# Six score bursts a batch in place of five, one of them inside a down pair

## The chip, the cores and the metric

The kernel runs on one core of one Trainium2 chip. Its time is the device time of one execution in microseconds (us); smaller is better. The engines are TensorE (PE, with its weight loads shown as PEld), VectorE (DVE), ScalarE (ACT), GpSimd (POOL) and SyncE (SP), each with its own queue of instructions, which it takes in order. Matmul results land in PSUM, which has eight banks.

## The reference

Sigmoid attention over 8 batches, 12 heads, 448 tokens and head size 64 is followed by a gated feed-forward network on all 3584 tokens (width 768, inner width 1536). Inputs and outputs are fp32; the kernel multiplies in fp16.

```python
scores = scale * np.matmul(q, k.transpose(0, 1, 3, 2)) - np.log(S)
attn = 1.0 / (1.0 + np.exp(-scores))
x = np.matmul(attn, v)              # then to (tokens, heads * head size)
gate = np.maximum(x @ w_gate, 0.0)
val = x @ w_val
out = gate * val @ w_out
```

There is no softmax, so a score needs one sigmoid and no sum over its row.

## The kernel before

**Attention.** A batch has three groups of four heads, and each group's keys come in seven chunks. A *unit* (`qk_unit`, line 292) is the scores of one group and one chunk: four 64x64 matmuls of 448 columns that run side by side in the four quarters of the array (`qk`, line 232). It fills two banks, and two sigmoids on ACT (line 187) carry them to an fp16 tile PT. A *value product* (`pv`, line 250) takes the seven PT tiles of one group: 28 such matmuls into two banks, which DVE scales and copies out as xT (line 184). A batch has 21 units, in order of group and chunk, and three value products.

**Bursts.** The units are cut into *bursts* by the list `cuts` (lines 699 to 706). Between bursts stands one piece of feed-forward work. `pv_at` names the bursts that hold a value product and the place in them: after two units of the burst. From batch 3 on there are five bursts, of 4, 4, 4, 4 and 5 units; the first, third and fifth hold a value product (the first one that of the last group of the batch before). Batch 2 has six bursts of 4, 3, 4, 3, 4 and 3 units, with the value products in those of four.

**Feed-forward work.** The first batches use plain products (`gv`, one strip of gate and value, line 309). From batch 2 on, work comes from a deque (`push_group`, line 668) that holds, for each two batches, six gate-and-value pairs, one plain down product (`down`, line 346) and three down pairs. `next_work` (line 682) takes one after each burst. Pairs form a 2x2 block product from seven smaller products in a reordered form (`gv_pair`, line 510; `down_pair`, line 423); sums of operands are made ahead on DVE by `prepare`, batch sums by `batch_sums`. With five pieces of work a batch, an even batch b gives y (the last down pair), w, w, w, w, and an odd one w, w, t, y, y; batch 3 has three plain strips, then t and y.

**A down pair** makes two tiles of 128 tokens, y1 and y2, from three banks b, c and a. Each product is six matmuls of 384 columns. In order: A11 x B11 into b, copied by DVE (line 416; ACT in the last pieces of the kernel) to the low half of y1; S1 x T1 into c, copied by ACT (line 421) to the high half of y2; S2 x T2 added into b, copied by ACT to the high half of y1; A12 x B21 into a, added to y1 low by DVE (line 437); S3 x T3 added into b, added to y2 high by DVE; S4 x B22 added into c, added to y1 high by DVE; the stores of y1; then A22 x T4 added into b, copied by ACT to the low half of y2; the stores of y2. The jobs handed in as `beside` follow the first copy: the DVE copies and SP transposes that bring the next keys and queries into place (`dma_transposes`, line 211), POOL's loads of the next batch, and batch sums.

**Banks.** `bank` (line 76) hands out the eight PSUM banks in a ring, the one that was given out longest ago first. `later` (line 84) moves banks to the ring's end by their place: the argument 7 is the last of the ring, 0 the first. A down pair ends with the order a, c, b behind the five others, a gate-and-value pair with a, a, c, c, b, b behind the two others. A matmul that writes a bank waits for the engine that read it last.

**Order.** The schedule is written by hand: instructions stand on each engine's queue in the order in which the program issues them.

Of the kernel before, what the change touches and what calls it, by code (L numbers as in the profile page):

```python
# [17 lines left out]
def kernel(  # L18
# [10 lines left out]
    nc = tc.nc  # L29

    B, H, S, D = q.shape
    DM, DF = moe_w_gate.shape
# [43 lines left out]
    def bank(name, shape=(P, 512), dtype=FP32):  # L76
        pool, tag = free[0]
        free.rotate(-1)
        return pool.tile(list(shape), dtype, tag=tag, name=name)
# [4 lines left out]
    def later(order):  # L84
        keys = [free[i - 8] for i in order]
        for key in keys:
            free.remove(key)
            free.append(key)
# [211 lines left out]
    def pv_group(b, g):  # L300
        pv(b, g, 0, S, [PT_tiles.pop((b, g, c))[:, :, 0:S] for c in range(NCH)])
# [32 lines left out]
    def store(g, t, ysb, m0, m1, engines):  # L334
        for i, eng in enumerate(engines):
            j = 2 * t + i
            b, c = 2 * g + j // NCH, j % NCH
            dst = out[b * S : (b + 1) * S, m0:m1].rearrange("(t c) m -> c t m", c=NCH)[c]
            eng.dma_start(dst, ysb[64 * i : 64 * i + 64, m0:m1])
# [24 lines left out]
    HF, HM, HD = NFC // 2, DM // 2, NDC // 2  # L364
# [55 lines left out]
    def scaled_act(o, ps):  # L420
        nc.scalar.activation(o, ps[:, 0:HM], AF.Copy, scale=OUT_SCALE)  # L421

    def down_pair(g, p, beside, then, last, first_copy):
        A11, A12, S3, A22 = token_blocks(g, p)
        S1, S2, S4 = sums.pop(("y", g, p))
        T1, T2, T3, T4 = (late["T"][:, i] for i in range(4))
        B11, B21, B22 = wo[:, 0:HF, 0:HM], wo[:, HF:NFC, 0:HM], wo[:, HF:NFC, HM:DM]
        y1, y2 = (ysbp.tile([P, DM], FP32, tag="ysb", name="ysb") for _ in range(2))
        lo, hi = slice(0, HM), slice(HM, DM)
        b, c, a = bank("u"), bank("y12"), bank("y11")  # L430
        later((7, 6, 5))

        def product(ps, A, W, first=True):
            products([(ps, HM, HF, A, W, first)])

        def plus(o, ps):
            nc.vector.scalar_tensor_tensor(  # L437
                out=o, in0=ps[:, 0:HM], scalar=OUT_SCALE, in1=o, op0=AOP.mult, op1=AOP.add
            )

        product(b, A11, B11)
        first_copy(y1[:, lo], b)
        beside()
        product(c, S1, T1)
        scaled_act(y2[:, hi], c)
        product(b, S2, T2, False)
        scaled_act(y1[:, hi], b)
        product(a, A12, B21)
        plus(y1[:, lo], a)
        if last:  # L450
            store(g, 2 * p, y1, 0, HM, (nc.sync, nc.sync))
        product(b, S3, T3, False)
        plus(y2[:, hi], b)
        if last:
            scaled_act(y2[:, lo], b)
            store(g, 2 * p + 1, y2, HM, DM, (nc.sync, nc.scalar))
        product(c, S4, B22, False)
        plus(y1[:, hi], c)
        if last:
            store(g, 2 * p, y1, HM, DM, (nc.sync, nc.scalar))  # L460
        else:
            store(g, 2 * p, y1, 0, DM, (nc.sync, nc.sync))
        then()
        if last:
            for m0 in (0, HM // 2):
                m1 = m0 + HM // 2
                d = bank("y21")
                products([(d, HM // 2, HF, A22, T4[:, :, m0:m1], True)])
                nc.vector.scalar_tensor_tensor(
                    out=y2[:, m0:m1], in0=d[:, 0 : HM // 2], scalar=OUT_SCALE, in1=y2[:, m0:m1],  # L470
                    op0=AOP.mult, op1=AOP.add,
                )
            store(g, 2 * p + 1, y2, 0, HM, (nc.sync, nc.scalar))
        else:
            product(b, A22, T4, False)
            scaled_act(y2[:, lo], b)
            store(g, 2 * p + 1, y2, 0, DM, (nc.sync, nc.sync))
# [165 lines left out]
    order = [(g, c) for g in range(NG) for c in range(NCH)]  # L643
# [12 lines left out]
    def both(b, g):  # L656
        pe_transposes(b, g, 0)
        pe_transposes(b, g, 1)
# [7 lines left out]
    work = deque()  # L666
# [12 lines left out]
            elif kind == "y":  # L679
                token_sums(g, i)  # L680

    def next_work(jobs=(), alone=False, first_act=False):
        kind, g, i = work.popleft()

        def beside():
            for job in jobs:
                job()

        if kind == "y":
            down_pair(g, i, beside, prepare, not work, scaled_act if alone or first_act else scaled)  # L690
        elif kind == "w":
            gv_pair(g, i, lambda: (prepare(), beside()), nc.scalar.copy if alone else nc.vector.tensor_copy)
        else:
            beside()
            prepare()
            down(g, i)

    ffn_mix(1, [(1, lambda: both(1, 0))])
    for b in range(1, B):
        if b == 1:  # L700
            cuts, pv_at = (0, 3, 6, 9, 13, 17, 21), {3: (0, 2), 5: (1, 2)}
        elif b == 2:
            cuts, pv_at = (0, 4, 7, 11, 14, 18, 21), {0: (-1, 2), 2: (0, 2), 4: (1, 2)}
        else:
            cuts, pv_at = (0, 4, 8, 12, 16, 21), {0: (-1, 2), 2: (0, 2), 4: (1, 2)}
        count = len(cuts) - 1
        hooks = {}
        if b == 1:
            mix = (3, 3, 3, 3, 3, 2)
            hooks = {  # L710
                1: [(1, lambda: both(1, 1))],
                3: [(1, lambda: both(1, 2))],
                4: [(3, lambda: dma_transposes(2, 0))],
                5: [(2, lambda: dma_transposes(2, 1)), (0, late_loads)],
            }
        elif b == 2:
            mix = (2, 2, 1, 1, 1, 2)
            hooks = {
                2: [(0, prepare)],
                4: [(0, lambda: weight_sums(0))],  # L720
                5: [(1, lambda: weight_sums(1)), (0, lambda: weight_sums(2))],
            }
            open_late()
        elif b == 3:
            mix = (1, 1, 1, 0, 0)
        else:
            mix = (0,) * count
        for m in range(count):
            jobs = []
            for i, (g, c) in enumerate(order[cuts[m] : cuts[m + 1]]):  # L730
                if m in pv_at and i == pv_at[m][1]:
                    if m == 0:
                        pv_finish(b - 1)
                        if b == 2:
                            push_group(0)
                        elif b % 2 == 0:
                            push_group(b // 2 - 1)
                    else:
                        pv_group(b, pv_at[m][0])
                qk_unit(b, g, c)  # L740
            if m == 0 and b > 2:
                jobs.append(lambda: dma_transposes(b, 2))
            if b == 2 and m == count - 1:
                jobs.append(lambda: (dma_transposes(3, 0), dma_transposes(3, 1)))
            elif b == 3 and m == count - 1:
                jobs.append(lambda: (dma_transposes(4, 0), dma_transposes(4, 1)))
            elif 0 <= m - count + 2 and 3 < b < B - 1:
                jobs.append(lambda: dma_transposes(b + 1, m - count + 2))
            if b == 1:
                if m == 0:  # L750
                    load(2, 0, 1, "kq")
                    load(2, 1, 2, "kq")
                    load(2, 2, 3, "kq")
                    load_v(2)
            elif m == 0 and b + 1 < B:
                if b == 3:
                    jobs.append(lambda: hold(3, 2))
                jobs.append(lambda: (load(b + 1, 0, 3, "kq"), load_v(b + 1)))
            if b % 2 and b > 2:
                if m == count - 1:  # L760
                    jobs.append(lambda: (batch_sums_t1(b // 2), batch_sums(b // 2, (0, 1))))
            elif b > 3 and m == 0:
                jobs.append(lambda: batch_sums(b // 2 - 1, (1, HD)))
            if b == 2 and m == count - 1:
                ffn_mix(mix[m], hooks[m])
                next_work(jobs + [lambda: weight_sums(3)], first_act=True)
            elif mix[m]:
                for job in jobs:
                    job()
                ffn_mix(mix[m], hooks.get(m, ()))  # L770
            else:
                next_work(jobs)
            if b == 3 and m in (1, 3):
                for f in range(*((0, 8, 2), (8, NFC, 2))[m // 2]):
                    gate_sums(f, f + 2)
# [35 lines left out]
```

## Time and profile before

| what | value |
|---|---|
| median of 3 runs | 396.19 us (396.19 to 396.75) |
| the profiled execution's own time | 396.35 us |
| its span, first to last instruction | 394.6 us |
| TensorE (PE) busy | 387.5 us, 98% |
| DVE busy | 279.8 us, 71% |
| ACT busy | 223.2 us, 57% |
| POOL busy | 49.5 us, 13% |
| mean granted TensorE clock | 0.998 |

A span is measured between the first and the last instruction on the core; the execution's own time has a little around it. A row of the timeline gives the start, the length, the engine, the line, the operation, out<-in by the program's names, and how many instructions were merged into it. Matmuls are pipelined: one starts before the one ahead of it has left the array, so the length of a row is longer than its share of the time, and the distance from one row's start to the next is what counts. In batches 4 to 7 bursts start at 126.73, 135.87, 144.99, 155.25, 164.39 (batch 4), 175.14, 185.40, 194.54, 200.75, 208.75 (batch 5), 218.39, 227.52, 236.64, 246.90, 256.04 (batch 6) and 266.80, 277.05, 286.20, 292.41, 300.40 (batch 7); batch 3 has 99.02, 103.60, 107.14, 111.93 and 117.10. The last value product is at 310.04; from there on only feed-forward work is left.

### The profile page before, as it was taken

The page shows a single profiled execution, that of the slowest core. Times are in us where ns is not written, and L with a number is a line of the kernel's source. Part 1 is how long each engine was busy: PE and PEld are TensorE (multiplying, and loading weights), DVE is VectorE, ACT ScalarE, POOL GpSimd, SP SyncE. Part 2 cuts the span into 40 slices and gives each one's busy share as a digit, 9 for nine tenths or more (in the row PEclk, how much of TensorE's full clock was granted, in tenths as well). Part 3 has the DMA queues.
Part 4 walks back from the last instruction along what each step waited for, and adds up shares of the span by engine and source line. Part 5 has one row for each costly group of instructions (what it writes and reads, how often), then busy time and mean ns, then how long its engine had stood idle before and what let it go on. Part 6 is the DMA issues. An engine that isn't in the chain of part 4 may idle for free.

```text
span 394.6 us, 8758 instructions
## 1 busy us (share of the span) xinstructions
PE 387.5 (98%) x3494; PEld 217.7 (55%) x3494; DVE 279.8 (71%) x540; ACT 223.2 (57%) x476; POOL 49.5 (13%) x73
## 2 busy tenths in 40 slices
PE   8999999999999999999999999999999999999995
PEld 3678786445455554554555545455455555555563
DVE  2453444367278899999758889999766779987663
ACT  5946778783886565655655555565566233543121
POOL 8634320500120300003000300000000000000000
PEclk9999999999999999999999999999999999999999
DMA  9999999998798891225945694223013320000135
GB/s 148 198 199 204 205 199 136 162 203 142 166 178 178 163 220 27 47 48 73 176 87 132 123 224 78 48 17 71 10 41 81 81 80 2 0 1 2 40 87 155
DMA packets 68953, 43.69 MB, mean 111 GB/s; under 512 B 35888, under 2 KB 65584, under 8 KB 68912
## 3 DMA queue, kind: packets, MB, share of 16 engines
q0 software_dynamic: 30736, 23.33, 39.5%
q1 hardware_dynamic: 37664, 19.24, 23.5%
q10 hardware_dynamic: 512, 0.56, 0.5%
q8 instruction: 27, 0.44, 0.4%
q14 instruction: 14, 0.11, 0.1%
HBM read 47.19 MB, written 11.01 MB: 147 GB/s over the span
## 4 chain that ended last, share of the span: by engine, by line
PE 91%; DMA 5%; POOL 1%; ACT 1%; issue 0%; DVE 0%; POOLq 0%; ACTq 0%
PE u L385 33%; PE g L385 16%; PE y L385 9%; PE qk_ps L232 8%; PE pv_ps L250 7%; PE g_ps L309 7%; PE v_ps L309 6%; DMA wv<-in_moe_w_val_dram 4%; PE ya L346 3%; DMA v<-in_v_dram 2%; PE yb L346 1%; PE trt L201 1%; ACT PT L187 1%; POOL k L110 1%; POOL q L110 1%
## 5 line engine op out<-in xcount | busy, mean ns | idle before, releaser
L187 ACT ACTIVATE PT<-qk_ps 128x448 f16<-128x448 f32 (+3 forms) x318 | 150.4, 595 | 70.4 <-PE qk_ps L232 70.3
L385 PEld LDWEIGHTS <-S 128*128 128x128 f16 x540 | 52.8, 98 | 43.6
L540 DVE TENSOR_TENSOR gsb<-g,gsb 128x448 f32<-128x448 f32 x72 | 42.9, 625 | 14.6 <-PE g L385 14.1
L232 PE MATMUL qk_ps<-qkT 64*64 64x448 f16 (+2 forms) x756 | 49.6, 336 | 0.8 <-DVE qkT L206 0.5
L421 ACT ACTIVATE ysb<-u 128x384 f32<-128x384 f32 x28 | 13.9, 497 | 55.5 <-PE u L385 53.4
L327 DVE TENSOR_TENSOR hT<-gate_sb,v_ps 128x256 f16<-128x256 f32 (+2 forms) x36 | 16.2, 465 | 35.5 <-ACT gate_sb L318 22.2
L536 ACT COPY gsb<-u 128x448 f32<-128x448 f32 x48 | 25.7, 566 | 23.9 <-PE u L385 22.9
L385 PEld LDWEIGHTS <-hT 128*128 128x128 f16 x294 | 28.1, 98 | 19.5 <-issue 2.1
L250 PE MATMUL pv_ps<-PT,v 64*64 64x448 f16 (+2 forms) x756 | 36.7, 329 | 0.0
L184 DVE TENSOR_SCALAR xT<-pv_ps 128x448 f16<-128x448 f32 (+2 forms) x53 | 27.9, 567 | 12.0 <-PE pv_ps L250 10.6
L309 PE MATMUL v_ps<-xT,wv 128*128 128x256 f16 (+2 forms) x216 | 33.3, 290 | 0.5 <-DMA wv<-in_moe_w_val_dram 0.4
L309 PE MATMUL g_ps<-xT,wg 128*128 128x256 f16 (+2 forms) x216 | 33.5, 291 | 0.1
L232 PEld LDWEIGHTS <-qkT 64*64 64x64 f16 x756 | 19.9, 105 | 24.7 <-issue 15.9
L385 PEld LDWEIGHTS <-wv 128*128 128x128 f16 x216 | 21.1, 98 | 19.7
L385 PEld LDWEIGHTS <-wg 128*128 128x128 f16 x216 | 20.3, 98 | 20.6 <-issue 3.0
L250 PEld LDWEIGHTS <-v 64*64 64x64 f16 x756 | 21.5, 107 | 11.1 <-issue 1.0
L385 PE MATMUL u<-T,hT 128*128 128x384 f16 x138 | 26.2, 326 | 0.0
L437 DVE SCALAR_TENSOR_TENSOR ysb<-y,ysb 128x384 f32<-128x384 f32 x24 | 13.4, 557 | 17.8 <-PE y L385 10.3
L309 PEld LDWEIGHTS <-wg 128*128 128x128 f16 x216 | 18.5, 98 | 11.5 <-issue 5.0
L110 POOL DMA_DIRECT2D k<-in_k_dram x14 | 10.9, 778 | 111.1 <-DVE rel L215 104.5
L309 PEld LDWEIGHTS <-wv 128*128 128x128 f16 x216 | 20.1, 98 | 8.4 <-DMA wv<-in_moe_w_val_dram 1.0
L385 PE MATMUL u<-xT,wg 128*128 128x448 f16 x108 | 23.5, 353 | 0.1
(69 smaller groups left out, 531.7 us busy)
## 6 DMA issues: line engine op xcount, KB each, us to landing
out_dram<-ysb SPq DMA_DIRECT2D x52, 192.0 KB, 2.9
k<-in_k_dram POOLq DMA_DIRECT2D x5, 672.0 KB, 11.7
q<-in_q_dram POOLq DMA_DIRECT2D x5, 672.0 KB, 14.6
v<-in_v_dram POOLq DMA_DIRECT2D x8, 336.0 KB, 14.7
v<-in_v_dram POOLq DMA_DIRECT2D x16, 168.0 KB, 13.9
k<-in_k_dram POOLq DMA_DIRECT2D x8, 224.0 KB, 12.0
wo<-in_moe_w_out_dram POOLq DMA_DIRECT2D x1, 1536.0 KB, 11.1
q<-in_q_dram POOLq DMA_DIRECT2D x6, 224.0 KB, 12.2
```

Source lines behind the costliest of these rows:

```text
L110: nc.gpsimd.dma_start(t16[:, xs, cs], rows_of(src, b)[:, xs, cs])
L184: nc.vector.tensor_scalar(out=xT, in0=src, scalar1=XSCALE, scalar2=None, op0=AOP.mult)
L187: nc.scalar.activation(PT_ap, ps_ap, AF.Sigmoid, bias=sig_bias, scale=qk_scale)
L232: nc.tensor.matmul(out_of(hh)[o : o + 64, :], qkT[rows, c, cols], qkT[rows, NCH + c0 : NCH + c1, cols], start=True, stop=True, tile_positi ...
L250: nc.tensor.matmul(ps[hh][64 * r : 64 * r + 64, 0:qn], v16[rows, 2 * g + hh, c * D : (c + 1) * D], pieces[c][rows, hh, :], start=(c == 0), ...
L309: nc.tensor.matmul(ps[-1][:, 0:qn], wt[:, dc, f * P : (f + 1) * P], xT_tiles[b][:, dc, q0 : q0 + qn], start=(dc == 0), stop=(dc == NDC - 1),)
L327: nc.vector.tensor_tensor(out=hT_tiles[g][:, f, o : o + qn], in0=gate_sb[:, 0:qn], in1=ps[1][:, 0:qn], op=AOP.mult,)
L346: nc.tensor.matmul(ps[:, 0 : m1 - m0], hT_tiles[g][:, f, t * P : (t + 1) * P], wo[:, f, m0:m1], start=(f == 0), stop=(f == NFC - 1),)
L385: nc.tensor.matmul(ps[:, 0:n], A[:, k_, :], W[:, k_, :], start=(first and k_ == 0), stop=(k_ == kn - 1), skip_group_check=True,)
L421: nc.scalar.activation(o, ps[:, 0:HM], AF.Copy, scale=OUT_SCALE)
L536: by(gs[u][i][:], ps[u][:, 0:S])
L540: nc.vector.tensor_tensor(out=gs[u][i][:], in0=ps[u][:, 0:S], in1=gs[u][i][:], op=AOP.add)
```

## The change

From batch 3 on, the cuts of batch 2 are used: six bursts of 4, 3, 4, 3, 4 and 3 units, with the value products in those of four. The pieces of feed-forward work stay five a batch, and so one burst stands inside a piece: in an even batch the second burst is issued inside the down pair after the first burst, in an odd batch the sixth inside the down pair after the fifth. In both cases it is a burst of three units without a value product.

A down pair with such an inner burst (argument `amid`) has another order. A11 x B11, S1 x T1 and S2 x T2 stay. S4 x B22 follows at once, then the inner burst, then S3 x T3, A12 x B21 and A22 x T4. The bank a is not taken at the start: `later((0,))` puts b at the ring's end after S3 x T3, so that A12 x B21 gets c's bank, and `later((6,))` puts b behind it again. The stores of y1 follow the adder of A12 x B21. The other down pairs are as before.

```diff
-    def down_pair(g, p, beside, then, last, first_copy):
+    def down_pair(g, p, beside, then, last, first_copy, amid=None):
...
-        b, c, a = bank("u"), bank("y12"), bank("y11")
-        later((7, 6, 5))
+        b, c = bank("u"), bank("y12")
+        if not amid:
+            a = bank("y11")
+            later((7, 6, 5))
...
-        product(a, A12, B21)
-        plus(y1[:, lo], a)
-        if last:
-            store(g, 2 * p, y1, 0, HM, (nc.sync, nc.sync))
-        product(b, S3, T3, False)
-        plus(y2[:, hi], b)
-        if last:
-            scaled_act(y2[:, lo], b)
-            store(g, 2 * p + 1, y2, HM, DM, (nc.sync, nc.scalar))
-        product(c, S4, B22, False)
-        plus(y1[:, hi], c)
+        if amid:
+            product(c, S4, B22, False)
+            plus(y1[:, hi], c)
+            amid()
+            product(b, S3, T3, False)
+            plus(y2[:, hi], b)
+            later((0,))
+            a = bank("y11")
+            later((6,))
+            product(a, A12, B21)
+            plus(y1[:, lo], a)
+        else:
...
-        elif b == 2:
+        else:
             cuts, pv_at = (0, 4, 7, 11, 14, 18, 21), {0: (-1, 2), 2: (0, 2), 4: (1, 2)}
-        else:
-            cuts, pv_at = (0, 4, 8, 12, 16, 21), {0: (-1, 2), 2: (0, 2), 4: (1, 2)}
-        count = len(cuts) - 1
+        bursts = list(range(len(cuts) - 1))
+        inner = None
+        if b > 2:
+            inner = 4 * (b % 2)
+            bursts.remove(inner + 1)
+        count = len(bursts)
...
+        def burst(n):
+            for i, (g, c) in enumerate(order[cuts[n] : cuts[n + 1]]):
+                if n in pv_at and i == pv_at[n][1]:
...
+                qk_unit(b, g, c)
+
+        for m in range(count):
+            jobs = []
+            burst(bursts[m])
...
-                next_work(jobs)
+                next_work(jobs, amid=(lambda: burst(inner + 1)) if m == inner else None)
```

The `else` branch holds the six lines of the old order.

## The prediction

> **What bounds the kernel now.** I read the page's busy table first, then the chain of waits, then the timeline of the tensor engine alone, because an engine that is always "busy" can still lose time between its matmuls.
>
> ```profile
> PE 387.5 (98%) x3494; PEld 217.7 (55%) x3494; DVE 279.8 (71%) x540; ACT 223.2 (57%) x476; POOL 49.5 (13%) x73
> PE 91%; DMA 5%; POOL 1%; ACT 1%; issue 0%; DVE 0%; POOLq 0%; ACTq 0%
> ```
>
> The tensor engine is the chain (91%); no other engine has a share worth chasing. So the time moves only by what the change does to the distances from one matmul's start to the next. Those are the starts in the timeline (first column), not the durations, which overlap.
>
> ```profile
> 69.26 0.76 PE L232 MATMUL qk_ps<-qkT 64*64 64x448 f16 x12
> 69.95 1.31 PE L309 MATMUL g_ps<-xT,wg 128*128 128x448 f16 x6
> ...
> 71.10 1.30 PE L309 MATMUL v_ps<-xT,wv 128*128 128x448 f16 x6
> 72.23 1.30 PE L309 MATMUL g_ps<-xT,wg 128*128 128x448 f16 x6
> 73.37 1.30 PE L309 MATMUL v_ps<-xT,wv 128*128 128x448 f16 x6
> 74.60 0.57 PE L232 MATMUL qk_ps<-qkT 64*64 64x448 f16 x8
> 75.00 1.49 PE L250 MATMUL pv_ps<-PT,v 64*64 64x448 f16 x28
> 76.33 0.55 PE L232 MATMUL qk_ps<-qkT 64*64 64x448 f16 x8
> 76.81 0.36 PE L309 MATMUL g_ps<-xT,wg 128*128 128x448 f16 x1
> ```
>
> This is batch 2, which already has the cuts that the change gives to batches 3 to 7. Three units without a value product (12 matmuls) take 69.95 - 69.26 = 0.69 us. Four units with one take 76.81 - 74.60 = 2.21. Six dense matmuls take 1.13 to 1.14 (71.10 to 72.23), but 1.23 when a burst follows (73.37 to 74.60), and 1.15 after one (69.95 to 71.10): a burst costs 0.09 + 0.01 = 0.10 outside itself.
>
> ```profile
> 154.83 1.15 DVE L545 SCALAR_TENSOR_TENSOR hT<-gsb,u 128x448 f16<-128x448 f32 x2
> 155.25 1.16 PE L232 MATMUL qk_ps<-qkT 64*64 64x448 f16 x16
> 156.34 1.31 PE L385 MATMUL u<-xT,wg 128*128 128x448 f16 x6
> ...
> 164.39 0.57 PE L232 MATMUL qk_ps<-qkT 64*64 64x448 f16 x8
> 164.79 1.49 PE L250 MATMUL pv_ps<-PT,v 64*64 64x448 f16 x28
> 166.12 1.04 PE L232 MATMUL qk_ps<-qkT 64*64 64x448 f16 x12
> 167.09 1.31 PE L385 MATMUL u<-xT,wg 128*128 128x448 f16 x6
> ```
>
> Batch 4, old cuts. Four units without a value product take 1.09; one more unit than 0.69 should cost 0.19 (four concurrent 448-column matmuls; six dense ones in 1.135 give 0.189 each), so 0.21 is lost. The reason is the ring of eight banks: four units want all eight, and the last two are those that the gate product read last. In the same timeline the fourth unit's last matmuls start at 156.03, just after the second gate product's end (154.83 + 1.15 = 155.98). Five units with a value product take 2.70 against 2.21 + 0.19 = 2.40: twelve banks are wanted, and the last unit waits 0.3 for sigmoids of the first ones.
>
> **The change, part by part.**
>
> *Cuts.* Bursts of 4, 4, 4, 4, 5 units become 4, 3, 4, 3, 4, 3, with the value products in the fours. The starts in the timeline give today's five bursts of each batch:
> batch 3: 2.21 + 1.16 + 2.42 + 1.17 + 2.70 = 9.66;
> batches 4 to 7: 2.21 + 1.09 + 2.21 + 1.09 + 2.70 = 9.30 each.
> New: 3 x 2.21 + 3 x 0.695 = 8.71, from the rows of batch 2. A three-unit burst needs six banks and leaves alone the two that were released last: after a gate-and-value pair the ring stands as two idle, a, c, b, and it stops before b; after a plain down product it stops before ya and yb. Inside are the same 84 score and 84 value matmuls of a batch; nothing is added but the sixth burst's own switches.
>
> *Sixth burst.* It stands inside a down pair, so 0.10 is added outside it. Its 0.13 inside (0.695 against 3 x 0.189) is in the 8.71 already. Batches 4 to 7 gain 9.30 - 8.71 - 0.10 = 0.49 each, 1.95 in all; batch 3 gains 9.66 - 8.81 = 0.85. Small change back: a product after a stalled four-unit burst had no 0.01 to pay in four places, 0.05 in all. **Sum: 2.75 us.**
>
> A rule speaks against a sixth burst. The Trainium skill's page TensorEngine Tiling (Tiling Modes) says "Changing tiling mode (not just tile) drains the TensorE", and TensorE: Matmul & The Clock Gate (Single matmul latency) puts a drain at about 175 ns. By those two, an estimate, a pair of switches is 0.35 where the rows above give 0.10 + 0.13 = 0.23, and the gain would be 2.15; the rows decide.
>
> *Order inside the pair.* S4 x B22 now follows S2 x T2 directly and adds into c, which the scalar engine has to have read. Today three products lie between the first product on c and the second (2.9 us); then one, 0.975.
>
> ```profile
> 221.58 1.14 PE L385 MATMUL y<-T,S 128*128 128x384 f16 x6
> 222.55 1.14 PE L385 MATMUL u<-T,S 128*128 128x384 f16 x6
> 222.80 0.49 ACT L421 ACTIVATE ysb<-y 128x384 f32<-128x384 f32 x1 [0.33 <-ACT PT L187]
> 223.53 1.14 PE L385 MATMUL y<-wo,hT 128*128 128x384 f16 x6
> ```
>
> This pair has the burst of four units before it that every pair with an inner burst will have. c is written at about 222.75, its copy ends at 223.29, and S4 x B22 would start at 223.53: 0.24 in hand, and the wait on the gate product above passed in 0.05. ACT had stood idle 0.33 before the copy, so it may come that much later and still be on time. Bounds: 0 as taken; if the last two sigmoids (8 in 3.60, 0.45 each) came 0.90 later, the copy would be 0.57 late and the product wait 0.57 + 0.05 - 0.24 = 0.38, in five pairs 1.9. I take 0, since the bursts' durations do not change. Behind a wait there would stand all of the tensor engine's queue.
>
> The inner burst writes the six banks that the burst before it used last; its sigmoids end 4.1 after that burst's start (218.39 to 222.48) and the inner burst starts 2.21 + 4 x 0.975 = 6.1 after it. S3 x T3 adds into b, whose copy ended before the inner burst. The last product but one takes c's bank: its adder on DVE is issued when S4 x B22 ends and has the burst and one product (1.7) for 0.56 of work; in even batches the X sums on DVE end about then (224.67 in this pair), leaving some 1.0. Its own adder for b has 0.975 against 0.26 + 0.56, as today. The value product that follows in the next burst needs the inner burst's six sigmoids: 0.35 + 2.7 = 3.1 against 0.70 + 3 x 0.975 + 0.09 + 0.40 = 4.1.
>
> *Queues.* The jobs beside the pair (input loads on POOL, transposes on SP) stay ahead of the inner burst. Only y1's two stores move back by the burst, 0.8 us, on SP; SP's next transposes are issued with the next pair. The stores land in 2.9 us and four ysb buffers cover two pairs of 7 us. I cost both at nothing. On ACT the six sigmoids push in between two copies of the pair, and the second, of the pair's last product, comes 3 us after the last of them.
>
> *DVE.* Its cover thins where gate-and-value pairs follow each other.
>
> ```profile
> 175.14:185.40 10.26, 10.26 (x88) 5.23 (x87) 10.00 (x20) 5.73 (x12) 3.66 (x5) 1.00 0.30 37
> 246.90:256.04 9.14, 9.14 (x59) 4.50 (x58) 8.94 (x18) 5.33 (x12) 0.00 (x0) 1.00 0.27 52
> ```
>
> These are busy times by stretch (length, then PE, weight loads, DVE, ACT, POOL). DVE has 10.00 of 10.26 us with a value product and the transposes' copies, and 8.94 in an interval that shrinks from 9.14 to 8.74. So it runs 0.2 late there and gets 0.26 back in the next. The first reader that could notice is the pair's last product, which waits for a sum that is done 0.8 before (183.34 against 184.17). Cost 0; bound: 0.2 in each of the two such intervals, 0.4.
>
> **The rivals.**
> 1. *The loss goes with the number of units in a row, not with banks.* Then the losses move with the units and only the sixth burst's switches are new: 5 x 0.23 = 1.15 slower, 397.3. Against it: 69.26 (three units, no loss beyond the switches) and the start at 156.03. It decides from the point where less than 1.15 of the lost 3.9 (2.75 + 1.15) goes away.
> 2. *c's copy comes late in the five pairs.* By the bound above 1.9 is given back, the gain is 0.85 and the time 395.3. For it: the room falls from 2.9 to 0.98. It would cancel the gain at a wait of 0.55 a pair.
> 3. *DVE becomes the pace between gate-and-value pairs,* 0.4 to twice that: 393.8 to 394.2.
> 4. *Batch 3 keeps its extra stalls.* A three-unit burst and the one gate-and-value unit behind it last 0.70 + 2.38 = 3.1 us there, and give ACT six sigmoids and a relu, 2.7 + 0.5 = 3.2. Price: all that batch 3 has today above the others, 9.66 - 9.30 = 0.36, so 393.8.
>
> **How the numbers follow.** The profiled execution took 396.35 with a span of 394.6; less 2.75 its time would be 393.6 and the span 391.8. The median of the runs was 396.19, 0.16 lower, so 393.4 there. Chances: forecast 0.72, rivals 3 and 4 together 0.12, rival 2 at part or all of its bound 0.09, rival 1 or another cost of that size 0.07. Changes under 0.2% (0.8 us) can't be told from none, so rival 2 is split: faster 0.88, same 0.05, slower 0.07. The range takes in rivals 3 and 4 and most of rival 2, up to 395.0; below, it goes 0.7 under the forecast, a little more than the spread of the runs shown (396.19 to 396.75): 392.7 to 395.0.
>
> **What would show it.** In the new timeline of batches 4 to 7: 12-matmul bursts of 0.69 to 0.70, none of 16 or of five units, fours with a value product 2.21; S4 x B22 and the inner burst without a longer step than 0.975 (plus 0.09 ahead of the burst). Wrong would be: a product of 1.1 or more ahead of S4 x B22 (rival 2), 12-matmul bursts near 0.9 (rival 1), or 1.135 steps that stretch in gate-and-value pairs (rival 3).

## The result and the profile after

The changed kernel takes 393.8 us (median of 6 runs, 393.23 to 393.97) against 396.19 us before (6 runs). The ratio is 0.9933 with a 95% interval of 0.9923 to 0.9943, which is 2.3 to 3.1 us faster. The forecast was 393.4 with a range of 392.7 to 395.0.

The profiled execution took 393.23 us with a span of 391.5. In the two traces, the stretch that the change touches goes from the first score matmul of batch 3 to the start of the last value product. It lasted 310.04 - 99.02 = 211.02 us before and 306.90 - 98.64 = 208.26 after: **2.76 us less, where the sum said 2.75.** The rest of the difference between the spans lies outside the change: batch 3 begins 0.38 earlier (the start-up differs from run to run), and the tail behind the last value product is the same, 84.5 and 84.6.

First the page after, its busy table and its chain:

```profile
PE 385.4 (98%) x3494; PEld 215.3 (55%) x3494; DVE 278.7 (71%) x540; ACT 224.8 (57%) x476; POOL 49.5 (13%) x73
PE 96%; ACT 2%; DVE 1%; issue 0%
```

The table hardly tells the two kernels apart: the largest differences are two microseconds of "busy" time of the tensor engine and of its weight loads. On the tensor engine that time was waiting under overlapping rows, not work: the count of matmuls is the same, 3494. The difference is in the timeline of the tensor engine. Batch 4 of the kernel after (start, length, engine, line, operation, tiles, shape, count):

```profile
144.46 1.30 PE L385 MATMUL u<-X,wv 128*128 128x448 f16 x6
145.69 0.76 PE L232 MATMUL qk_ps<-qkT 64*64 64x448 f16 x12
146.38 1.31 PE L385 MATMUL u<-xT,wg 128*128 128x448 f16 x6
147.53 1.30 PE L385 MATMUL g<-X,S 128*128 128x448 f16 x6
...
154.43 0.57 PE L232 MATMUL qk_ps<-qkT 64*64 64x448 f16 x8
154.84 1.49 PE L250 MATMUL pv_ps<-PT,v 64*64 64x448 f16 x28
156.16 0.55 PE L232 MATMUL qk_ps<-qkT 64*64 64x448 f16 x8
156.64 0.55 PE L385 MATMUL u<-xT,wg 128*128 128x448 f16 x2
```

From start to start: a burst of three takes 0.69, one of four with a value product 2.21, the product ahead of a burst 1.23 and the one behind it 1.15. Every burst of batches 3 to 7 has these lengths, and the products of 384 columns beside a burst take 1.07 ahead of it and 0.985 behind it in place of 0.975. Away from bursts, six matmuls of 448 columns take 1.135, six of 384 columns 0.975, twelve of 512 columns 2.60 and twelve of 256 columns 1.31. If all matmuls of the stretch followed each other at these steps, and the score and value matmuls, four abreast, at that of one of 448 columns, it would be 6.9 us shorter. A burst costs 0.23 for its two *switches*, from the full array to 64x64 tiles and back, and 30 of them make 6.9. So by this sum no wait is left on the tensor engine in this stretch, only switches. The steps away from bursts are the same in both traces, so the granted clock (0.998 before, 1.000 after) is not the difference.

The down pair with the inner burst, batch 4:

```profile
128.69 1.14 PE L385 MATMUL y<-T,S 128*128 128x384 f16 x6
129.67 1.14 PE L385 MATMUL u<-T,S 128*128 128x384 f16 x6
129.87 0.49 ACT L421 ACTIVATE ysb<-y 128x384 f32<-128x384 f32 x1 [0.28 <-PE y L385]
130.64 1.14 PE L385 MATMUL y<-wo,S 128*128 128x384 f16 x6
131.71 0.76 PE L232 MATMUL qk_ps<-qkT 64*64 64x448 f16 x12
132.41 1.15 PE L385 MATMUL u<-T,hT 128*128 128x384 f16 x6
```

The copy of c ends at 130.36 and S4 x B22 starts at 130.64, one product's step (0.975) behind S2 x T2. It waits for nothing.

### The profile page after: what moved, and what is told of

The parts are those of the page before. It is cut to its first block, busy times and chain, and to the rows that moved or that the text cites. A ratio compares the mean times of both kernels' runs of the same rounds, so it can differ in the third digit from the quotient of the medians.

```text
span 391.5 us, 8755 instructions
## 1 busy us (share of the span) xinstructions
PE 385.4 (98%) x3494; PEld 215.3 (55%) x3494; DVE 278.7 (71%) x540; ACT 224.8 (57%) x476; POOL 49.5 (13%) x73
## 4 chain that ended last, share of the span: by engine, by line
PE 96%; ACT 2%; DVE 1%; issue 0%
PE u L385 33%; PE g L385 16%; PE qk_ps L232 9%; PE y L385 9%; PE pv_ps L250 8%; PE g_ps L309 8%; PE v_ps L309 7%; PE ya L346 3%; ACT PT L187 2%; PE yb L346 1%; PE trt L201 1%; PE warm_ps L175 1%; DVE qkT L206 0%; DVE ysb L483 0%; DVE zeros L129 0%
## 5 line engine op out<-in xcount | busy, mean ns | idle before, releaser
L232 PE MATMUL qk_ps<-qkT 64*64 64x448 f16 (+2 forms) x756 | 47.3, 335 | 0.9 <-DVE qkT L206 0.5
L232 PEld LDWEIGHTS <-qkT 64*64 64x64 f16 x756 | 17.8, 105 | 21.8 <-issue 13.5
```

The costliest lines, as they stand in the source:

```text
L232: nc.tensor.matmul(out_of(hh)[o : o + 64, :], qkT[rows, c, cols], qkT[rows, NCH + c0 : NCH + c1, cols], start=True, stop=True, tile_positi ...
```

## What the lost 0.2 us was: four runs on the kernel before

The sum was right, but its reason deserved a test. The prediction said that a burst of four units without a value product loses 0.21 us because its fourth unit waits for the bank that the gate product still reads. A closer look at the kernel before speaks against that in one place. Behind the plain down product no gate product is near, and the loss is the same. These rows are from the timelines of DVE, ACT and the tensor engine there:

```profile
200.75 0.97 PE L232 MATMUL qk_ps<-qkT 64*64 64x448 f16 x16
200.86 0.42 DVE L353 TENSOR_SCALAR ysb<-yb 128x256 f32<-128x256 f32 x1 [0.51 <-PE yb L346]
201.24 0.54 ACT L187 ACTIVATE PT<-qk_ps 128x448 f16<-128x448 f32 x1 [2.61 <-PE qk_ps L232]
201.84 0.48 PE L385 MATMUL u<-wo,hT 128*128 128x384 f16 x2
```

The last reader of the fourth unit's bank ends at 201.28, 0.53 into the burst, in time for the fourth unit (at 0.59). The burst's first sigmoid ends at 201.78, and the next dense product starts at 201.84. This suggested theory B: four units hold all eight banks, so the *product behind the burst* waits for the first bank to come back, and that is the end of the first sigmoid. Theory A is the prediction's, and theory C is its first rival (the loss goes with the number of units). Each of the four kernels below ran once; the kernel before took 396.77 us beside them. The start-up alone differs by about a microsecond between these runs, and so the stretch of the trace is compared and not the time.

**Take away the gate product's read.** One line in `gv_pair`:

```diff
-            gated(u, 0, gs[u][0][:], b[u][:, 0:S])
+            gated(u, 0, gs[u][0][:], gs[u][1][:])
```

> The kernel before, but the first gate product of a gate-and-value pair reads a copy in SBUF (the sum kept for the other half) in place of the value bank b, so nothing reads b after its last product; one of the pair's two value factors is thereby replaced by another, the amount of work stays. Looked at: the bursts of four units without a value product in batches 4 to 7, from their first score matmul to the first dense matmul behind them. There are four behind a gate-and-value pair (1.09 us today), two behind a down pair (1.08) and two behind the plain down product (1.08). Theory A, the prediction's: the fourth unit waits for the gate product to release b. Then the four behind a gate-and-value pair fall to 0.88 and the other four stay, 0.8 us in all. Theory B: the dense matmul behind the burst waits for the first sigmoid of the burst, because the burst holds all eight banks. Then all eight stay at 1.08 to 1.09 and the time stays, though the fourth unit of the four bursts starts whole at 0.59. Theory C (the loss goes with the number of units): all stay, and the fourth unit's start too.

The four bursts behind gate-and-value pairs fell from 1.09 or 1.10 us to 1.08, not to 0.88; the other four stayed. The time was 395.99 us; the stretch took 210.91 against 211.02. In the first of them:

```profile
155.06 0.95 PE L232 MATMUL qk_ps<-qkT 64*64 64x448 f16 x16
155.55 0.54 ACT L187 ACTIVATE PT<-qk_ps 128x448 f16<-128x448 f32 x1 [4.39 <-PE qk_ps L232]
156.14 0.35 PE L385 MATMUL u<-xT,wg 128*128 128x448 f16 x1
```

The merged row of the burst is 0.95 long where it was 1.16: the fourth unit's four matmuls now start together at 0.59 (they were at 0.59 and 0.78). Still the next product starts at 156.14, just behind the sigmoid's end (155.55 + 0.54 = 156.09). So theory A's wait existed, but without it the burst won 0.01 in place of 0.21. Theory C falls as well: it had the fourth unit's start unchanged.

**Give the first bank back sooner.**

```diff
         for hh in range(2):
-            sigmoid(PT[:, hh, 0:S], ps[hh][:, 0:S])
+            n = 64 if short and hh == 0 else S
+            sigmoid(PT[:, hh, 0:n], ps[hh][:, 0:n])
...
-                qk_unit(b, g, c)
+                qk_unit(b, g, c, short=b > 2 and m in (1, 3) and i == 0)
+            if b > 2 and m in (1, 3):
+                g, c = order[cuts[m]]
+                sigmoid(PT_tiles[(b, g, c)][:, 0, 64:S], PT_tiles[(b, g, c)][:, 1, 64:S])
```

> The kernel before, but in a burst of four units without a value product (from batch 3 on) the first sigmoid covers 64 of its 448 columns; the other 384 are filled behind the burst's last sigmoid from the second half of the same tile, so those scores are not the right ones. The first bank is thereby given back about 0.32 us earlier (384 columns at the 0.83 ns each that a 448-column sigmoid's 0.423 us step and 0.545 us length allow at most). Theory A: no change, 1.08 to 1.09 everywhere. Theory B: the two bursts behind the plain down product fall to 0.88, the two behind a down pair to 0.93 (their fourth unit waits until 0.65 for the last copy of the pair), the four behind a gate-and-value pair only to 1.07 (their fourth unit waits until 0.78): 0.8 us in all. Theory C: no change.

Behind the plain down product 0.90 (expected 0.88), behind down pairs 0.96 (0.93), behind gate-and-value pairs 1.09 (1.07). The pattern is theory B's, each value a few hundredths longer:

```profile
155.16 1.16 PE L232 MATMUL qk_ps<-qkT 64*64 64x448 f16 x16
156.25 0.36 PE L386 MATMUL u<-xT,wg 128*128 128x448 f16 x1
...
200.60 0.96 PE L232 MATMUL qk_ps<-qkT 64*64 64x448 f16 x16
201.03 0.22 ACT L187 ACTIVATE PT<-qk_ps 128x64 f16<-128x64 f32 x1 [2.61 <-PE qk_ps L232]
201.50 0.34 PE L386 MATMUL u<-wo,hT 128*128 128x384 f16 x1
```

The time was 395.75 us; the stretch took 210.57, 0.45 less. The four bursts that moved gave 0.61 together. Three bursts of five units gave 0.06 each, one burst of batch 3 took 0.06 more, and two later products lost 0.12 each. In the first of these two, the extra sigmoid that fills the tile stands on ACT ahead of the down pair's copies, from 204.12 to 204.72; the copy of b ends at 205.48, and the product that needs b starts at 205.53.

**Both at once.**

> Both of the last two edits in one kernel, with what each leaves out. Theory A: 0.88 behind gate-and-value pairs, 1.08 elsewhere, 0.8 us less. Theory B: 0.88 behind gate-and-value pairs and behind the plain down product, 0.93 behind down pairs: 4 x 0.21 + 2 x 0.15 + 2 x 0.20 = 1.5 us less. Theory C: nothing moves.

```profile
155.99 0.95 PE L232 MATMUL qk_ps<-qkT 64*64 64x448 f16 x16
156.87 0.36 PE L386 MATMUL u<-xT,wg 128*128 128x448 f16 x1
...
201.05 0.96 PE L232 MATMUL qk_ps<-qkT 64*64 64x448 f16 x16
201.95 0.34 PE L386 MATMUL u<-wo,hT 128*128 128x384 f16 x1
```

Now all four bursts behind gate-and-value pairs take 0.88, behind down pairs 0.96 and behind the plain down product 0.90. The time was 395.94 us; the stretch took 209.80, 1.2 less than before, where 1.5 was expected; the same two later products give 0.23 of that back. So behind a gate-and-value pair *two* waits stood side by side. Theory A's alone lets the next product start at 1.09 (the run with the early bank), theory B's alone at 1.08 (the run without the gate product's read), and only taking both away brings it to 0.88. Behind the plain down product theory B's stood alone. Behind a down pair the fourth unit waits for the pair's last copy, but with the early bank the next product still starts at 0.96, so that wait is the shorter one. A burst of three units has neither: it leaves two of the eight banks to the next product, and all 15 of them take 0.69.

**The new order of products, without a burst in it.** The old cuts, with the down pair in the order of `amid` and nothing issued in its middle. Against the kernel after:

```diff
+        elif b == 2:
+            cuts, pv_at = (0, 4, 7, 11, 14, 18, 21), {0: (-1, 2), 2: (0, 2), 4: (1, 2)}
         else:
-            cuts, pv_at = (0, 4, 7, 11, 14, 18, 21), {0: (-1, 2), 2: (0, 2), 4: (1, 2)}
+            cuts, pv_at = (0, 4, 8, 12, 16, 21), {0: (-1, 2), 2: (0, 2), 4: (1, 2)}
...
-            bursts.remove(inner + 1)
...
-                next_work(jobs, amid=(lambda: burst(inner + 1)) if m == inner else None)
+                next_work(jobs, amid=(lambda: None) if m == inner else None)
```

> The change's new order of products in the five down pairs alone, with the old cuts and nothing issued in the pair's middle. The prediction costed the order at nothing: the copy of c has 0.975 us and takes 0.25 + 0.49, also behind the burst of five units that three of the five pairs then have in front. So the products of these pairs keep a step of 0.975, and the time is that of the kernel before, within 0.2 us of span outside the first 99 us. Rival 2 of the prediction: S4 x B22 is held up, and the product ahead of it takes up to 0.38 longer in each of five pairs, up to 1.9 us in all.

The stretch took 211.71, 0.69 *more*; the time was 397.3 against 396.77. The products of the pairs did keep their step of 0.975, also behind five units. Three products of the pair in batch 5:

```profile
214.06 1.14 PE L385 MATMUL u<-T,S 128*128 128x384 f16 x6
215.04 1.14 PE L385 MATMUL y<-wo,S 128*128 128x384 f16 x6
216.01 1.14 PE L385 MATMUL u<-T,hT 128*128 128x384 f16 x6
```

The loss is in the bursts behind four of the five pairs: +0.27 in two and +0.07 in two. The first of them, with a row of ACT between those of the tensor engine:

```profile
127.03 0.57 PE L232 MATMUL qk_ps<-qkT 64*64 64x448 f16 x8
127.13 0.49 ACT L421 ACTIVATE ysb<-u 128x384 f32<-128x384 f32 x1 [3.41 <-PE u L385]
127.67 1.52 PE L250 MATMUL pv_ps<-PT,v 64*64 64x448 f16 x28
...
129.50 1.15 PE L385 MATMUL u<-wo,hT 128*128 128x384 f16 x6
```

It takes 129.50 - 127.03 = 2.47 in place of 2.21, and its value product starts just behind the end of the copy (127.13 + 0.49 = 127.62). The expectation had overlooked that `later((0,))` finds the bank b at the ring's head only because the inner burst has turned the ring by six banks. Without the burst it moves another bank. Then b, which the pair's last copy reads until 0.60 us into the next burst, stands fifth in the ring and not last, and the value product or the third unit waits for it. So order and inner burst are one edit: the order costs the pair's products nothing, but its bank calls only fit with the burst.

## What the inner burst needs: four runs on the kernel after

**The inner burst behind its pair and not inside.**

```diff
-                next_work(jobs, amid=(lambda: burst(inner + 1)) if m == inner else None)
+                next_work(jobs)
+                if m == inner:
+                    burst(inner + 1)
```

> The changed kernel, but the inner burst is issued behind its down pair (in the old order of products) and not inside it, so that it meets the next burst: seven units and a value product in a row, sixteen banks' worth through eight. By the bank theory these bursts run at ACT's pace, about 0.43 us a sigmoid: the seventh unit needs the bank of the fourth, whose sigmoids end at 0.45 + 8 x 0.43 = 3.9 us, and the product behind it that of the fifth, some 0.4 later. So about 4.5 us in place of 0.70 + 2.21 + 0.23 outside and inside for one pair of switches: 1.4 us a batch in four batches, and in the fifth the burst only meets the last value product. The kernel would be 5 to 6 us slower than the changed one and 2.5 to 3.5 slower than the one before. If units in a row cost by their number alone (theory C), it would save the switches, 0.2 a batch, and be about 1 us faster than the changed one.

401.33 us, ratio to the kernel before 1.0132 (1.0117 to 1.0147): 7.5 slower than the changed kernel, more than expected. A merged burst in this kernel:

```profile
125.33 1.90 PE L232 MATMUL qk_ps<-qkT 64*64 64x448 f16 x20
127.29 1.95 PE L250 MATMUL pv_ps<-PT,v 64*64 64x448 f16 x28
128.89 0.96 PE L232 MATMUL qk_ps<-qkT 64*64 64x448 f16 x8
129.91 1.14 PE L385 MATMUL u<-wo,hT 128*128 128x384 f16 x6
...
313.56 3.05 PE L250 MATMUL pv_ps<-PT,v 64*64 64x448 f16 x28
316.54 0.66 PE L385 MATMUL u<-wo,hT 128*128 128x384 f16 x3
```

The merged burst takes 129.91 - 125.33 = 4.58 where 4.5 was expected. The expectation set this against 0.70 + 2.21 + 0.23, but the 0.13 of the switches inside a burst is already in the first two; against 0.69 + 2.21 + 0.10 a batch loses 1.6 and not 1.4. And it missed the price of the last one: the final value product follows the inner burst at once, waits for its sigmoids and takes 316.54 - 313.56 = 2.98 in place of 1.45. The same cuts thus make the kernel slower or faster, depending on whether some dense products (here three, 2.9 us) stand between the sixth burst and the next. Theory C, which had this kernel faster, falls here too.

**The price of one more burst.** The inner burst in two parts, each with its own pair of switches:

```diff
-            amid()
+            amid(0, 2)
             product(b, S3, T3, False)
             plus(y2[:, hi], b)
+            amid(2, 3)
...
-        def burst(n):
+        def burst(n, i0=0, i1=None):
             for i, (g, c) in enumerate(order[cuts[n] : cuts[n + 1]]):
+                if i < i0 or (i1 is not None and i >= i1):
+                    continue
...
-                next_work(jobs, amid=(lambda: burst(inner + 1)) if m == inner else None)
+                next_work(jobs, amid=(lambda i0, i1: burst(inner + 1, i0, i1)) if m == inner else None)
```

> The changed kernel with its inner burst in two parts: two units where it stands, the third behind S3 x T3. That is one more pair of mode switches in each of five pairs and nothing else. By the prediction's price, 0.10 outside and 0.13 inside a burst, 5 x 0.23 = 1.15 us more than the changed kernel. By the drains that the skill's pages state (0.35 a pair of switches, an estimate) 1.75 more.

394.81 us, ratio to the kernel before 0.9968 (0.9957 to 0.9979), so 1.0 slower than the changed kernel by the medians. In the trace the stretch is 209.78, 1.52 more: 5 x 0.23 = 1.15 as priced, and 0.36 in a single place, the first burst of batch 4. First the inner burst in two parts, in batch 3:

```profile
122.72 0.57 PE L232 MATMUL qk_ps<-qkT 64*64 64x448 f16 x8
123.22 1.15 PE L385 MATMUL u<-T,hT 128*128 128x384 f16 x6
124.30 0.38 PE L232 MATMUL qk_ps<-qkT 64*64 64x448 f16 x4
124.62 1.15 PE L385 MATMUL y<-wo,hT 128*128 128x384 f16 x6
125.60 1.14 PE L385 MATMUL u<-T,hT 128*128 128x384 f16 x6
```

That is 125.60 - 122.72 = 2.88, where the kernel after takes 0.69 + 0.985 + 0.975 = 2.65. Then the single place: the timelines of SP in the kernel after and in this one, and the burst in this one:

```profile
120.19 4.07 SPq L219 DMA_TRANSPOSE qkT<-rel  x2
```

```profile
121.12 5.07 SPq L219 DMA_TRANSPOSE qkT<-rel  x2
127.03 0.38 PE L232 MATMUL qk_ps<-qkT 64*64 64x448 f16 x4 [0.29 <-DMA qkT<-rel]
```

The first score matmul there waits for the first of two transposes, the one that brings batch 4's first keys and queries. It landed at 126.99, 5.87 us after its issue. In the kernel after it landed 5.13 us after its issue, at 125.31, and the burst starts at 125.50 without a wait: 0.19 us in hand. The loads of batch 4's values landed until 124.49 in the run with two parts and until 122.69 in the kernel after; whether they held the transpose up is not shown. The switches themselves cost 0.23 a pair, as the rows of batch 2 had it. The Trainium skill's page TensorE: Matmul & The Clock Gate (Single matmul latency) puts the drain of a single matmul at about 175 ns beside its streaming time. Taken twice for each of the five bursts, an estimate, that would have been 1.75 in place of 1.15; the trace decides.

**How much later the copy of c may come.**

```diff
+        late["junk"] = pool.tile([P, S], FP16, tag="junk", name="junk")
+        nc.gpsimd.memset(late["junk"][:], 0.0)
...
         product(c, S1, T1)
+        for _ in range(2 if amid else 0):
+            sigmoid(late["junk"][:], late["junk"][:])
         scaled_act(y2[:, hi], c)
```

The other kernel has 1 in place of 2.

> The changed kernel with one more 448-column sigmoid (on a scratch tile, nothing reads it) on ACT just ahead of the copy of c in each of the five pairs with an inner burst. The copy stands idle 0.28 us before it starts in the changed kernel, and S4 x B22 starts 0.28 after the copy's end. One sigmoid of 0.43 to 0.48 puts the copy 0.15 to 0.20 later: no loss, the same time as the changed kernel, within its noise.

> The same with two more sigmoids. The copy starts 0.58 to 0.68 later and S4 x B22 0.35 to 0.45 later: about 2.0 us more than the changed kernel over five pairs, most of the gain. That is the price that the prediction gave its rival 2 (0.38 a pair, 1.9 in all). If the pair had more room than the timeline shows, nothing would be lost.

With one sigmoid more: 393.84 us (393.53 to 394.12), the stretch 208.35 against 208.26. No loss in the pairs: the 0.09 stands ahead of batch 4's first burst, which starts 0.04 behind the landing of the same transpose as in the run with two parts, here 5.36 us after its issue. But the copy did not come 0.15 to 0.20 later, as was expected. In all five pairs it starts 0.20 behind S2 x T2, where the kernel after has 0.20 in four pairs and 0.25 in one. The sigmoid fits into the time in which ACT stood idle, and the copy ends 0.21 to 0.22 ahead of S4 x B22 in place of 0.24 to 0.28. With two: 395.81 us, ratio to the kernel before 0.9990 (0.9981 to 0.9999), and the stretch 210.44, 2.18 more or 0.44 a pair. In the kernel with two, rows of the tensor engine and then of ACT:

```profile
130.47 1.14 PE L387 MATMUL u<-T,S 128*128 128x384 f16 x6
131.88 1.14 PE L387 MATMUL y<-wo,S 128*128 128x384 f16 x6 [0.27 <-ACT ysb L423]
...
130.19 1.26 ACT L187 ACTIVATE junk<-junk 128x448 f16<-128x448 f16 x2
131.35 0.47 ACT L423 ACTIVATE ysb<-y 128x384 f32<-128x384 f32 x1
```

S4 x B22 now names the copy as its releaser and starts at 131.88, 0.06 behind the copy's end and 1.41 behind the product before it. So the new order has room for one more sigmoid, with less than 0.2 us left over: at two, four fifths of the gain are gone.

## Why the prediction was right, point by point

- *The cuts.* Right in every row: 0.69 and 2.21 in all 30 bursts, batch 3 included, so rival 4 (batch 3 keeps extra stalls) did not occur. Reading the new bursts' lengths from batch 2 of the kernel before carried the sum.
- *The reason for the lost 0.21.* Only partly right. That four units take all eight banks holds. That the fourth unit waits for the gate product holds too, but only in four of the eight bursts, and there it ends 0.01 after a second wait that the prediction did not see: the product behind the burst needs the first bank, and so the end of the first sigmoid. In the other four bursts that second wait set the end. The row at 156.03, just after 155.98, showed one wait and made it look sufficient; the two bursts behind the plain down product, in the same timeline, would have shown the other. The sum did not suffer, since three units have neither wait. That they are free of the second one was not reasoned out beforehand; it was in the measured rows of batch 2.
- *The five units' 0.30.* It is gone with them. The cause it was put down to, sigmoids of the first units, was not tested apart, but the traces agree. In batch 4 of the kernel before, the second unit's last sigmoid ends 2.34 into the burst and the rest of the fifth unit starts at 2.39. In the run with the early bank the two come at 2.28 and 2.33.
- *The sixth burst's 0.23.* Confirmed by splitting the inner burst.
- *The order in the pair, costed at nothing (rival 2).* Confirmed by the rows of the pair. In the kernel after the copy starts 0.20 to 0.25 behind S2 x T2, with 0.24 to 0.28 in hand at its end. The bound was 0.38 a pair for two sigmoids more; the run with two measured 0.44. There the two added sigmoids span 1.26 us and put the copy 0.69 later, where the bound had 0.57.
- *DVE (rival 3).* It did not become the pace. The busy times of the short interval with the transposes' copies:

```profile
164.69:173.43 8.74, 8.74 (x55) 4.29 (x54) 8.69 (x18) 4.46 (x10) 0.00 (x0) 1.00 0.29 54
```

DVE has 8.69 of 8.74 us there, so the cover is as good as used up. The overshoot of 0.2 that was worked out from 8.94 did not come: the same 18 instructions stand back to back and overlap more at their ends (pairs of 1.15 us start 1.07 apart), and their busy time is 0.25 shorter.
- *The transposes, costed at nothing with the other queues.* That held, but narrowly: the one that batch 4's first burst needs landed 0.19 us ahead of it. With one sigmoid more in the pairs the burst waited 0.09, with the inner burst in two parts 0.36. The prediction had not looked at this margin.
- *Rival 1* (the loss goes with the units) is out: four units in a row take 0.88 when both waits are taken away.
- *The time.* 2.75 was forecast, the stretch shows 2.76, the ratio says 2.3 to 3.1. The agreement to 0.01 is that of one pair of traces; the medians differ by 2.4. The median of 393.8 is 0.4 over the forecast, inside the spread of the runs.

## What to carry to other kernels

When a burst fills a ring of buffers, look at the instruction *behind* the burst as well as at the last one in it: it needs the buffer that the burst filled first, and so waits for the first evacuation, however early the others end. Where two waits end within a few hundredths of each other, neither shows its worth alone; take away both before a cause is named. And a stage of the same kernel that already runs with the new sizes (here batch 2) gives prices that hold even where the reason for them is only half understood.

## What was not expected

- A burst costs 0.23 us at its two changes between 64x64 tiles and the full array, the same in every one of 30 bursts to a hundredth. What in the change takes the time is not shown. By the sum above it is all that the tensor engine loses in 208 us. To save more of it there would have to be fewer bursts, none of them waiting for its banks.
- Bank calls that count places in a ring tie pieces of code together that look independent: the pair's new order without the inner burst lost 0.69 us.
- The transpose that batch 4's first burst needs landed 5.13 us after its issue in the kernel after, 5.36 with one sigmoid more and 5.87 with the inner burst in two parts, right at the start of that burst.
